# Loading two weight matrices from GpSimd's DMA queue with the fp16 conversion in the transfer

## The chip, the cores and the metric

One core of one Trainium2 chip runs the whole program. The metric is device time in microseconds, the median of the runs. Inputs and output are fp32 in DRAM; the matmuls work on bf16 and fp16 tiles on the chip.

## The reference, cut to what matters

Attention with a decay per position feeds a gated convolutional feed-forward block. Eight batches, eight heads, 576 positions, head size 64, so d_model is 512 and d_ff is 1024.

```python
scores = scale * q @ k.T                          # per batch and head, 576 x 576
decay  = cumsum(log(clip(f)))[:, None] - cumsum(log(clip(f)))[None, :]
attn   = softmax(where(causal, -1e9, scores + decay))
x      = (attn @ v)                               # heads side by side: [8, 576, 512]
h      = maximum(x @ w_in, 0)                     # [8, 576, 1024]
conv   = sum(conv_w[k] * h shifted by k - 1, k = 0..2)
out    = (h * sigmoid(conv)) @ w_out              # [8, 576, 512]
```

`w_in` is 512 x 1024 and `w_out` 1024 x 512, each 2 MB in fp32. Both are read once and used for all eight batches.

## The kernel before, in words

Everything is done on the one core in one pass. The attention is worked in 16 half batches of four heads (hb 0 to 15), the feed-forward in 8 batches (b 0 to 7), each as soon as its two half batches are through. The order of all work is written out by hand: the string ORDER lists some thousand steps, and each engine and each DMA queue gets its instructions in the order in which the steps stand there. An instruction waits only for its own data, but what stands behind it on its engine waits with it.

The steps that matter here, by their names in ORDER:

- `q2.0`, `q3.1` and the like (L233) load q or k of one half batch by a transposing DMA on SP's queue into one of four `qk` tiles. `cl` (L239, VectorE) then repairs the rows that carry the decay, and `rw` (L255, L256, SP) writes the decay rows into the tile.
- `v1.0` to `v1.4` (L262, SP) load v of batch 1 in five pieces into one of two `vf` tiles. `va2.0` and `va2.1` (L270, L272) convert them to fp16 on whichever engine ORDER names: `@POOL`, `@DVE` or `@ACT`.
- `sd`, `st`, `so` are score matmuls (L362, masks by L370), `ed`, `et`, `eo` the exponentials on ScalarE (L403, L382, L420).
- `pv` (L444, L448) is attention times v, `n` (L456, L458, VectorE) divides by the sums, `t` (L465, L467) turns the result, `tx` (L475) copies it out of PSUM.
- `f` (L484) is the first feed-forward matmul, `r` (L496) the relu, `c` and `d` (L503, L505) the convolution, `a` (L508) the tanh, `g` (L512) the gate, `o` (L523) the second matmul, `e` (L529) its eviction to an `ob` tile and `s` (L557) the store.
- `ki` (L328) and `zc` (L332, L333) are small DMAs on GpSimd's queue that write the decay rows and constants to DRAM.

The weights come in eight pieces of 512 KB: `wi0` to `wi3` for w_in and `wo0` to `wo3` for w_out. Each piece is loaded in fp32 into one of the three `ob` tiles by a DMA on SP's queue (`stage`, L571), and then converted into its half of `w_in_f16` or `w_out_f16` by `stage_cast` (L579): six of the eight casts stand on GpSimd (`wic0`, `wic1`, `wic2`, `woc1`, `woc3`, `woc2`), one on VectorE (`wic3`) and one on ScalarE (`woc0`). A piece of w_in holds two of the four row blocks for half of the columns: `f0.0` to `f0.3` need `wi0` and `wi1`, `f0.4` to `f0.7` need `wi2` and `wi3`. A piece of w_out holds two of the eight row blocks: `o0.0` starts with the blocks of `wo0` and needs all four pieces.

Of the kernel before, what the change touches and what calls it, by code (L numbers as in the profile page):

```python
# [19 lines left out]
q2.1 cl1.0.1@DVE cw ed0 cl1.1.1@DVE so0.1 v0.2 rw1 so0.0 eo0.0 q2.0 sd1 eo0.1 so1.0 ed1 cl2.1 cwt v0.4 wi3@SP eo1.0  # L20
va1.0@DVE sd3 ed3 cl2.0 sd2 st0 ed2 so2.0 va0.0@POOL va0.1@POOL eo2.0 q3.0 so2.1 wi0@SP wic0@POOL so1.1 eo2.1 so3.0
cl3.0 wic3@DVE so3.1 et0 va1.1@DVE eo1.1 rw2 pv0.0 eo3.1 st1 pv0.1 et1 sd4 q3.1 n0.0 n0.1 t0 wi1@SP eo3.0 pv1.0 q5.0
tx0@ACT pv1.1 cl3.1 n1.0 sd5 ed4 so5.0 n1.1 t1 tx1@DVE wic1@POOL so5.1 so4.1 wi2@SP rw3 ed5 eo5.1 f0.0 so4.0 q5.1
eo5.0 r0.0@ACT f0.1 st2 v1.0 q4.0 cl5.0 eo4.1 c0.0 d0.0 v1.2 eo4.0 r0.1@ACT f0.2 c0.1 v1.1 et2 sd6 cl5.1 r0.2@ACT c0.2
ed6 d0.1 h0 wic2@POOL a0.0 f0.3 so6.1 rw5 d0.2 eo6.1 r0.3@ACT a0.1 g0.0 c0.3 a0.2 g0.2 f0.4 f0.5 f0.6 f0.7 r0.5@ACT
v1.3 va2.0@POOL q4.1 r0.4@ACT sd7 so7.1 c0.5 cl4.0 c0.4 d0.4 ed7 so7.0 g0.1 r0.6@ACT eo7.1 sd10 so6.0 v1.4 eo7.0
wo2@SP r0.7@DVE eo6.0 a0.4 sd11 d0.3 so10.1 ed11 va3.0@POOL pv3.0 cl4.1 ed10 eo10.1 st3 d0.5 c0.6 so11.0 et3 wo1@SP
n3.0 a0.5 rw4 so11.1 wo3@SP va3.1@ACT pv2.0 eo11.1 c0.7 va2.1@POOL eo11.0 q6.0 pv2.1 v2.0 q6.1 woc1@POOL n2.0 n2.1
d0.7 sd9 ed9 pv3.1 so10.0 n3.1 a0.3 t2 wo0@SP g0.3 sd8 eo10.0 ed8 a0.7 t3 so9.0 v2.3 tx2@DVE tx3@DVE st5 eo9.0 g0.4
st4 d0.6 g0.5 v2.2 f1.0 et4 et5 so8.0 g0.7 f1.1 cl6.0 v2.1 r1.0@ACT eo8.0 woc3@POOL so8.1 c1.0 woc2@POOL f1.2 a0.6  # L30
cl6.1 v2.4 r1.1@ACT eo8.1 f1.3 v3.0 d1.0 r1.2@ACT g0.6 h1 r1.3@DVE a1.0 k0@POOL f1.4 so9.1 f1.5 rw6 q7.0 woc0@ACT zc
# [79 lines left out]
def kernel(  # L111
# [11 lines left out]
    nc = tc.nc  # L123
# [75 lines left out]
    add = plan.add  # L199
# [564 lines left out]
```

## Time and profile before

| what | value |
|---|---|
| median of three runs | 250.42 us (249.34 to 254.94) |
| span of the profiled execution | 246.3 us |
| median less span | 4.1 us |
| TensorE busy, matmul | 227.3 us, 92% |
| VectorE busy | 218.8 us, 89% |
| ScalarE busy | 209.2 us, 85% |
| GpSimd busy | 66.7 us, 27% |
| granted TensorE clock | full, in all slices |
| weight DMAs on SP's queue | 8, of 512 KB each |
| packets on the software queue (GpSimd's) | 304, 0.73 MB |

The page gives the span of the profiled execution and no separate time for it; the three runs lie around a median 4.1 us above that span. The profile names a tile by the kernel's names, "SPq" and "POOLq" are the queues' sequencers, q1 is the hardware DMA queue that SP feeds and q0 the software queue that GpSimd feeds. The number in square brackets behind a row of a timeline is the time in which the engine sat idle before it, and what ended that.

### The profile page before, as it was taken

Reading aid. Unit: us, or ns where it says so; the run is one execution under the profiler, and the core shown is the slowest. Engines: PE = TensorE matmul, PEld = TensorE weight load, DVE = VectorE, ACT = ScalarE, POOL = GpSimd, SP = SyncE. Lnnn points to the kernel's source line nnn. Section 1 sums busy time; section 2 is a strip of 40 time slices with the busy share of each in tenths; the row PEclk is TensorE's granted clock in tenths of the full one; section 3 lists DMA queues with packets and bytes.
Section 4 is the critical chain, followed back from the end, with each engine's and each line's share of the span. In section 5 each row is a group of like instructions: output and inputs, shape, how many; then the busy total and the mean of one; then the engine's idle time right before and its main releaser. Section 6 shows DMA issues by size and latency. Waiting matters only on the chain.

```text
span 246.3 us, 6458 instructions
## 1 busy us (share of the span) xinstructions
PE 227.3 (92%) x2644; PEld 145.0 (59%) x2644; DVE 218.8 (89%) x334; ACT 209.2 (85%) x282; POOL 66.7 (27%) x94
## 2 busy tenths in 40 slices
PE   0889979978999999989999999999999999999993
PEld 0777765557656755666557666665566566544441
DVE  6846285999998999999999999999999999999972
ACT  3558849999998999999999999989998999869641
POOL 8302022033423310550625244045234022001110
PEclk9999999999999999999999999999999999999999
DMA  6998999999999979899999999999999506334336
GB/s 163 335 238 195 225 204 212 225 179 287 210 238 226 231 169 213 165 230 225 237 230 225 243 235 205 185 245 192 280 208 198 159 1 92 104 118 170 101 124 202
DMA packets 116421, 48.80 MB, mean 198 GB/s; under 512 B 106290, under 2 KB 106546, under 8 KB 116392
## 3 DMA queue, kind: packets, MB, share of 16 engines
q1 hardware_dynamic: 115778, 47.24, 89.1%
q0 software_dynamic: 304, 0.73, 1.0%
q10 hardware_dynamic: 310, 0.42, 0.6%
q8 instruction: 20, 0.33, 0.6%
q14 instruction: 9, 0.07, 0.1%
HBM read 21.11 MB, written 10.17 MB: 127 GB/s over the span
## 4 chain that ended last, share of the span: by engine, by line
PE 49%; DVE 17%; ACT 14%; DMA 8%; issue 5%; SPq 4%; POOL 1%; ACTq 0%; DVEq 0%
PE ps L523 16%; PE ps L484 16%; PE ps L362 9%; DVE hg L512 4%; PE ps L444 4%; ACT pp L420 4%; DMA qk<-in_q_dram 3%; DVE u L505 3%; DVE u L503 3%; DMA vf<-in_v_dram 3%; ACT ht L496 3%; SPq L233 2%; DVE qk L227 2%; DMA hg<-in_q_dram 2%; DVE xm L458 2%
## 5 line engine op out<-in xcount | busy, mean ns | idle before, releaser
L484 PE MATMUL ps<-xt,w_in_f 128*128 128x512 f16 (+1 forms) x512 | 69.3, 286 | 0.3 <-DVE xt L475 0.3
L420 ACT ACTIVATE pp<-ps 128x1024 f16<-128x1024 f32 x64 | 64.5, 1035 | 4.2 <-PE ps L367 2.8
L362 PE MATMUL ps<-qk 128*128 128x128 bf16 (+2 forms) x576 | 62.1, 240 | 2.9 <-DVE xm L458 1.4
L523 PE MATMUL ps<-w_out_f,hg 128*128 128x512 f16 x256 | 59.9, 379 | 0.4 <-ACT ht L496 0.2
L505 DVE SCALAR_TENSOR_TENSOR u<-ht,cwt,u 128x576 f32<-128x576 f16 x64 | 53.7, 850 | 0.5
L503 DVE SCALAR_TENSOR_TENSOR u<-ht,cwt 128x576 f32<-128x576 f16 x64 | 52.2, 831 | 2.0 <-ACT ht L496 1.8
L508 ACT ACTIVATE hg<-u,cw 128x576 f16<-128x576 f32 x64 | 49.5, 788 | 4.5 <-DVE u L505 4.5
L362 PEld LDWEIGHTS <-qk 128*128 128x128 bf16 x576 | 38.7, 98 | 20.7 <-issue 4.5
L512 DVE SCALAR_TENSOR_TENSOR hg<-hg,ht 128x576 f16<-128x576 f16 x64 | 50.6, 811 | 0.3 <-POOL pt L385 0.3
L484 PEld LDWEIGHTS <-w_in_f 128*128 128x128 f16 x512 | 34.0, 98 | 28.1 <-issue 0.4
L523 PEld LDWEIGHTS <-hg 128*128 128x128 f16 x256 | 23.9, 98 | 26.6 <-issue 0.6
L496 ACT ACTIVATE ht<-ps 128x576 f16<-128x576 f32 x55 | 35.8, 665 | 1.8 <-PE ps L484 1.1
L406 POOL TENSOR_SCALAR_AFFINE_SELECT pp<-pd 128x1024 f16<-128x1024 f32 x20 | 25.3, 1279 | 43.1 <-ACT pd L403 34.4
L444 PE MATMUL ps<-va,pp 128*128 128x65 f16 x640 | 24.6, 193 | 1.3 <-POOL va L270 0.9
L458 DVE TENSOR_TENSOR xm<-ps,rc 128x896 f16<-128x896 f32 (+1 forms) x32 | 24.3, 758 | 1.1
L444 PEld LDWEIGHTS <-pp 128*128 128x128 f16 x640 | 22.7, 97 | 3.6 <-issue 1.7
L403 ACT ACTIVATE pd<-ps 128x1024 f32<-128x1024 f32 x20 | 20.3, 1026 | 1.7 <-issue 1.1
L239 DVE TENSOR_SCALAR qk<-qk,lim 128x2304 uint16<-128x2304 uint16 x12 | 10.8, 906 | 10.0 <-DMA qk<-in_q_dram 7.6
L529 ACT COPY ob<-ps 128x1024 f32<-128x1024 f32 (+1 forms) x17 | 16.1, 947 | 1.6 <-PE ps L523 1.3
L385 POOL TENSOR_SCALAR_AFFINE_SELECT pt<-p 128x256 f16<-128x256 f32 x10 | 8.4, 854 | 26.8 <-ACT p L382 19.6
L517 POOL COPY tl<-hg 128x64 f16<-128x64 f16 (+1 forms) x6 | 4.2, 694 | 38.1 <-DVE hg L512 38.1
L403 ACT ACTIVATE pp<-ps 128x1024 f16<-128x1024 f32 x12 | 12.1, 1030 | 1.7 <-PE ps L362 1.7
(93 smaller groups left out, 212.3 us busy)
## 6 DMA issues: line engine op xcount, KB each, us to landing
vf<-in_v_dram SPq DMA_DIRECT2D x32, 256.0 KB
out_dram<-ob SPq DMA_DIRECT2D x14, 512.0 KB
qk<-blank SPq DMA_DIRECT2D x8, 540.0 KB
ob<-in_moe_w_in_dram SPq DMA_DIRECT2D x4, 512.0 KB
ob<-in_moe_w_out_dram SPq DMA_DIRECT2D x4, 512.0 KB
vf<-in_v_dram SPq DMA_DIRECT2D x8, 128.0 KB
out_dram<-ob SPq DMA_DIRECT2D x8, 128.0 KB
out_dram<-ob SPq DMA_DIRECT2D x3, 256.0 KB
```

The lines of the kernel that those rows point to most:

```text
L362: nc.tensor.matmul(o, tk[:, h * S + k0:h * S + k0 + 128], tq[:, h * S + q0:h * S + q0 + n], start=first, stop=last and not by_matmul(hb, h))
L403: nc.scalar.activation(o, ps_of(f"sd{i}").rearrange("p (s c) -> p s c", s=2), AF.Exp, scale=SCALE)
L420: nc.scalar.activation(pair(i)[:, s, 512:1536], ps_of(f"so{i}.{s}"), AF.Exp, scale=SCALE)
L444: nc.tensor.matmul(ps[:, c:c + D + 1], block(hb, h, m, n), va[:, h, m, 0:D + 1], start=(m == 0), stop=(m == n))
L458: nc.vector.tensor_tensor(x.rearrange("p (j h d) -> p j h d", j=a, d=D), got[:, :, :, 0:D], r.unsqueeze(3).broadcast_to((128, a, g, D)), o ...
L484: nc.tensor.matmul(ps[:, c:c + n], w_in_f16[:, cc, 128 * ff:128 * (ff + 1)], xt[:, cc // 2, x:x + n], start=(cc == 0), stop=(cc == NCC - 1))
L496: nc.scalar.activation(o, i, AF.Relu, scale=0.5)
L503: nc.vector.scalar_tensor_tensor(u, ht[:, 0:S], cwt[:, ff, 0:1], ht[:, 1:1 + S], op0=ALU.mult, op1=ALU.add)
L505: nc.vector.scalar_tensor_tensor(u, ht[:, 2:2 + S], cwt[:, ff, 1:2], u, op0=ALU.mult, op1=ALU.add)
L508: nc.scalar.activation(hg_of(b, ff), u_t[slot[f"c{b}.{ff}", "u"]], AF.Tanh, scale=cw[:, ff, 1:2])
L512: nc.vector.scalar_tensor_tensor(hv, hv, 1.0, ht_of(b, ff)[:, 1:1 + S], op0=ALU.add, op1=ALU.mult)
L523: nc.tensor.matmul(ps[:, 512 * (c % 2):512 * (c % 2 + 1)], w, w_out_f16[:, ff, :], start=(ff == 0), stop=(ff == NFF - 1))
```

## The change

The eight steps `wi0` to `wi3` and `wo0` to `wo3` become DMAs on GpSimd's queue that read fp32 from DRAM and write fp16 straight into the weight tiles. The eight casts and their use of the `ob` tiles are gone. The matmuls wait for the DMAs themselves instead of the casts. V is loaded and converted as it was. In ORDER the steps keep their places; `wic` and `woc` are struck out.

```diff
-    def stage(w, j, e):
-        ob = ob_t[slot[f"{w}{j}", "ob"]].rearrange("p j c -> p (j c)").rearrange("p (x c) -> p x c", x=2)
+    def load_w(w, j):
         if w == "wi":
-            src = moe_w_in.rearrange("(cc p) ff -> p cc ff", p=128)[:, 2 * (j % 2):2 * (j % 2) + 2,
-                                                                    512 * (j // 2):512 * (j // 2) + 512]
+            x, y = 2 * (j % 2), 512 * (j // 2)
+            nc.gpsimd.dma_start(w_in_f16[:, x:x + 2, y:y + 512],
+                                moe_w_in.rearrange("(cc p) ff -> p cc ff", p=128)[:, x:x + 2, y:y + 512])
         else:
-            src = moe_w_out.rearrange("(ffc p) dm -> p ffc dm", p=128)[:, 2 * j:2 * j + 2, :]
-        queue(e).dma_start(ob, src)
-
-    def stage_cast(w, j, e):
...
-        {"ACT": nc.scalar.copy, "POOL": nc.gpsimd.tensor_copy, "DVE": nc.vector.tensor_copy}[e](dst, ob)
+            nc.gpsimd.dma_start(w_out_f16[:, 2 * j:2 * j + 2, :],
+                                moe_w_out.rearrange("(ffc p) dm -> p ffc dm", p=128)[:, 2 * j:2 * j + 2, :])
...
-            add(f"{w}{j}", "SP/POOL/ACT", [], lambda e, w=w, j=j: stage(w, j, e), take=["ob"])
-            add(f"{w}c{j}", "POOL/ACT/DVE", [f"{w}{j}"], lambda e, w=w, j=j: stage_cast(w, j, e), give=[("ob", f"{w}{j}")])
+            add(f"{w}{j}", "POOL", [], lambda w=w, j=j: load_w(w, j))
...
-            add(f"f{b}.{ff}", "PE", [f"tx{2 * b}", f"tx{2 * b + 1}"] + [f"wic{2 * (ff // 4) + j}" for j in range(2)],
+            add(f"f{b}.{ff}", "PE", [f"tx{2 * b}", f"tx{2 * b + 1}"] + [f"wi{2 * (ff // 4) + j}" for j in range(2)],
...
-        wo = [f"woc{j}" for j in range(4)]
+        wo = [f"wo{j}" for j in range(4)]
```

Three places show how the instructions move; line numbers are those of each kernel, the new one being two lines shorter up to the weight functions and eleven behind them. The first is SP's queue from the load of q for half batch 3 (`q3.0`, into qk_88) to the first loads of v for batch 1 (vf_90); ob_130 to ob_132 are the three fp32 tiles. Before:

```order
L571 DMA ob_130<-in_moe_w_in_dram 128x2x512
L233 DMA_TRANSPOSE qk_88<-in_q_dram 128x2304
L571 DMA ob_131<-in_moe_w_in_dram 128x2x512
L255 DMA qk_87<-image 1x2304
L256 DMA qk_87<-image 2x2304
L233 DMA_TRANSPOSE qk_88<-in_k_dram 128x2304
L571 DMA ob_132<-in_moe_w_in_dram 128x2x512
L233 DMA_TRANSPOSE qk_86<-in_q_dram 128x2304
L571 DMA ob_131<-in_moe_w_in_dram 128x2x512
```

And now:

```order
L231 DMA_TRANSPOSE qk_88<-in_q_dram 128x2304
L253 DMA qk_87<-image 1x2304
L254 DMA qk_87<-image 2x2304
L231 DMA_TRANSPOSE qk_88<-in_k_dram 128x2304
L231 DMA_TRANSPOSE qk_86<-in_q_dram 128x2304
```

Four weight loads are gone from between the loads of q and k. The four of w_out are gone in the same way further down that queue.

The second place is GpSimd's own order, from `ki` through the conversions of v for batch 0 (into va_92) and batch 1 (into va_93 and va_94) to the last of the weight steps. Before:

```order
L328 DMA image<-kc 64x576 x3
L270 CAST va_92<-vf_89 128x4x4x64
L272 CAST va_92<-vf_89 64x4x64
L579 CAST w_in_f_69<-ob_131 128x2x512
L579 CAST w_in_f_69<-ob_132 128x2x512
L579 CAST w_in_f_69<-ob_131 128x2x512
L270 CAST va_93<-vf_90 128x4x4x64
L270 CAST va_94<-vf_90 128x4x4x64
L272 CAST va_93<-vf_90 64x4x64
L579 CAST w_out_f_70<-ob_132 128x1024
L579 CAST w_out_f_70<-ob_131 128x1024
L579 CAST w_out_f_70<-ob_130 128x1024
```

And now:

```order
L326 DMA image<-kc 64x576 x3
L565 DMA w_in_f_69<-in_moe_w_in_dram 128x2x512
L268 CAST va_92<-vf_89 128x4x4x64
L270 CAST va_92<-vf_89 64x4x64
L565 DMA w_in_f_69<-in_moe_w_in_dram 128x2x512 x3
L268 CAST va_93<-vf_90 128x4x4x64
L568 DMA w_out_f_70<-in_moe_w_out_dram 128x2x512
L268 CAST va_94<-vf_90 128x4x4x64
L568 DMA w_out_f_70<-in_moe_w_out_dram 128x2x512 x2
L270 CAST va_93<-vf_90 64x4x64
L568 DMA w_out_f_70<-in_moe_w_out_dram 128x2x512
```

`wi3` now goes out right behind `ki`; `wi0`, `wi1`, `wi2` stand behind the two conversions of v for batch 0; `wo2` stands between `va2.0` (va_93) and `va3.0` (va_94), `wo1` and `wo3` ahead of `va2.1`, and `wo0` behind it.

The third place is VectorE from `cl3.0` (into qk_88) over `va1.1` (into va_91) to the first `n` step (`n0.0`, into xm_109). Before:

```order
L239 TENSOR_SCALAR qk_88<-qk_88,lim 128x2304
L579 CAST w_in_f_69<-ob_130 128x2x512
L272 CAST va_91<-vf_89 64x4x64
L456 RECIPROCAL rc_111<-ps_136 128x14
L458 TENSOR_TENSOR xm_109<-ps_136,rc_111 128x896
```

And now:

```order
L237 TENSOR_SCALAR qk_88<-qk_88,lim 128x2304
L270 CAST va_91<-vf_89 64x4x64
L454 RECIPROCAL rc_111<-ps_136 128x14
L456 TENSOR_TENSOR xm_109<-ps_136,rc_111 128x896
```

The cast of the weights between `cl3.0` and `va1.1` is gone; the rest keeps its order.

109 lines of the change are left out of this document (51 added, 58 removed).

## The prediction

> **What bounds the kernel now.** I read the busy time of each engine in stretches first, to see where an engine still idles.
>
> ```profile
> span 246.3 us, 6458 instructions
> 20.00:30.00 10.00, 9.86 (x128) 7.43 (x126) 3.84 (x10) 9.08 (x12) 1.43 (x2) 1.00 1.02 226
> 30.00:40.00 10.00, 8.10 (x145) 6.09 (x145) 7.08 (x13) 6.17 (x8) 2.12 (x2) 1.00 1.05 214
> 40.00:50.00 10.00, 9.99 (x93) 5.84 (x92) 9.04 (x12) 9.40 (x15) 1.50 (x1) 1.00 1.02 204
> 50.00:60.00 10.00, 7.98 (x135) 5.88 (x134) 9.56 (x13) 9.88 (x14) 3.47 (x4) 1.00 0.99 240
> 60.00:70.00 10.00, 9.55 (x138) 6.61 (x131) 9.90 (x17) 9.40 (x14) 3.58 (x3) 1.00 1.16 223
> 70.00:80.00 10.00, 9.45 (x107) 5.66 (x106) 8.99 (x14) 8.94 (x12) 3.68 (x7) 1.00 1.16 223
> 110.00:130.00 20.00, 20.00 (x207) 12.07 (x205) 19.55 (x28) 19.36 (x27) 5.54 (x5) 1.00 1.17 233
> ```
>
> The columns behind the length are the busy times of TensorE (PE), its weight loads, VectorE (DVE), ScalarE (ACT) and GpSimd (POOL), then granted clock, DMA share and GB/s. From 110 us on TensorE has no gap, and VectorE and ScalarE hardly any: nothing that this change touches works there, and a lead or a delay from before is carried to the end. All that can be won lies in the gaps from 20 to 80 us, where TensorE is idle for 60 less 54.9, or 5.1 us. DMA is busy throughout, and GpSimd is idle over 60% of each stretch, so its six casts cost nothing by their own length.
>
> Next I looked at who ends the gaps. The largest single one is at 32 us, and VectorE makes it:
>
> ```profile
> 33.26 0.78 PE L465 MATMUL ps<-ident,xm 128*128 128x128 f16 x8 [1.30 <-DVE xm L458]
> 29.40 0.88 DVE L239 TENSOR_SCALAR qk<-qk,lim 128x2304 uint16<-128x2304 uint16 x1 [5.99 <-DMA qk<-in_q_dram]
> 30.20 0.69 DVE L579 CAST w_in_f<-ob 128x1024 f16<-128x1024 f32 x1
> 30.80 1.13 DVE L272 CAST va<-vf 64x256 f16<-64x256 f32 x1
> 31.85 0.23 DVE L456 RECIPROCAL rc<-ps 128x14 f32<-128x14 f32 x1
> ```
>
> TensorE waits 1.30 us for `n0.0`. VectorE had been held 5.99 us by the load `q3.0`, then did the weight cast `wic3`, then `va1.1`, and only then `n0.0`.
>
> **The change part by part.** *VectorE at 30 us.* `wic3` goes: 0.69 us. `va1.1` also shortens, for it took four times its usual length while GpSimd cast `wic0` beside it:
>
> ```profile
> L272 DVE CAST va<-vf x3: 281/281/1127, 30.8 to 157.7; 64x256 f16<-64x256 f32 x3
> 30.70 1.09 POOL L579 CAST w_in_f<-ob 128x1024 f16<-128x1024 f32 x1 [6.86 <-DMA ob<-in_moe_w_in_dram]
> ```
>
> 1.13 less 0.28 is 0.85 us. Together `n0.0` comes 1.54 us earlier if `q3.0` lands when it did, and TensorE gains its whole idle 1.30 us.
>
> *SP's queue.* Eight issues leave it:
>
> ```profile
> L571 SPq DMA_DIRECT2D ob<-in_moe_w_in_dram x4: 524/586/620, 20.8 to 36.7; - x4
> L571 SPq DMA_DIRECT2D ob<-in_moe_w_out_dram x4: 399/567/683, 54.0 to 66.5; - x4
> 20.84 0.62 SPq L571 DMA_DIRECT2D ob<-in_moe_w_in_dram x1
> 21.51 4.26 SPq L233 DMA_TRANSPOSE qk<-in_q_dram  x1
> ```
>
> At the medians that is 4 x 0.586 + 4 x 0.567 = 4.6 us, 2.3 of it ahead of v for batch 1. `q3.0` goes out 0.67 us earlier and no longer behind 512 KB of `wi3`; but `wi3` now shares the DMA engines with the first loads of v, and `wi0` to `wi2` with `q3.0` and `q3.1`. I take these as even and leave `q3.0` where it was.
>
> *GpSimd's queue.* The nearest rows for an issue there are of 64 pieces of 1152 bytes each; the weights have 256 pieces of 2 KB.
>
> ```profile
> L328 POOL DMA_DIRECT2D image<-kc x3: 523/528/717, 7.9 to 9.1; - x3
> 53.36 2.55 POOL L270 CAST va<-vf 128x1024 f16<-128x1024 f32 x2 [9.73 <-DMA vf<-in_v_dram]
> 55.97 1.15 PE L444 MATMUL ps<-va,pp 128*128 128x65 f16 x32 [0.93 <-POOL va L270]
> ```
>
> An issue lies between 0.52 us (the row) and 2.1 us (four times it, by pieces). I take 1.0, an estimate nearer to the row, since one instruction's fixed part isn't paid per piece. This is no idle engine's own affair at one place: `wo2` now stands between `va2.0` and `va3.0`, and `pv3.0` already waited 0.93 us for `va3.0`. So `pv3.0` starts at 55.97 - d + i, where d is how much earlier v of batch 1 lands (0 if the DMA engines are the limit, 2.3 if SP's issues are; I take 2.0, because SP goes from one issue straight to the next, as from 20.84 over 21.46 to 21.51 above) and i the issue. That is 54.97, a lead of **1.0 us** of the 1.3; with the ends it runs from 1.8 us lead to 2.1 us loss.
>
> *ScalarE at 72 us.* `woc0` goes, 1.03 us, but ScalarE waited shortly after it:
>
> ```profile
> 72.39 1.03 ACT L579 CAST w_out_f<-ob 128x1024 f16<-128x1024 f32 x1
> 75.10 1.05 ACT L270 CAST va<-vf 128x1024 f16<-128x1024 f32 x1 [0.77 <-DMA vf<-in_v_dram]
> 78.52 0.82 DVE L503 SCALAR_TENSOR_TENSOR u<-ht,cwt 128x576 f32<-128x576 f16 x1 [0.94 <-ACT ht L496]
> ```
>
> If v for batch 2 doesn't land earlier, the cast becomes a longer wait and the gain is 0; if it does, 1.03 + 0.77 = 1.8 us. `wo1`, `wo3` and `wo0` leave SP ahead of it (about 1.7 us of issues). I take **0.5**, since VectorE has only its own 0.94 us of idle time to follow with.
>
> *When the weights land.* They must be there at these places:
>
> ```profile
> 39.05 1.14 PE L484 MATMUL ps<-xt,w_in_f 128*128 128x512 f16 x8
> 45.12 4.08 PE L484 MATMUL ps<-xt,w_in_f 128*128 128x512 f16 x32
> 73.47 3.61 PE L523 MATMUL ps<-w_out_f,hg 128*128 128x512 f16 x16 [0.16 <-ACT w_out_f L579]
> 23.44 0.40 POOL L272 CAST va<-vf 64x256 f16<-64x256 f32 x1 [2.40 <-DMA vf<-in_v_dram]
> 7.89 1.75 POOL L328 DMA_DIRECT2D image<-kc  x3 [0.99 <-DVE kc L322]
> ```
>
> `wi0` goes out at 23.8. The software queue is slow to start: of `ki`, issued from 7.89, the first packets ran in the 12th microsecond. I allow 2.5 us. `f0.0` needs 1.05 MB in 39.05 - 26.3 = 12.8 us, `f0.4` 1.57 MB in 18.8 us: 82 and 84 GB/s. `wo2` goes out behind `va2.0` at about 54.6, data from 57.1; `o0.0` needs 2.10 MB in 16.4 us: **128 GB/s**. What the queue moves beside transposes:
>
> ```profile
> q0 software_dynamic: 18, 0.05, 17.9%
> q0 software_dynamic: 37, 0.10, 30.8%
> q0 software_dynamic: 177, 0.43, 30.0%
> q0 software_dynamic: 74, 0.21, 70.3%
> ```
>
> These are packets, MB and share of the DMA engines in the windows 11 to 12, 12 to 13, 75 to 80 and 79 to 80 us: 100, 86 and at best 210 GB/s once running. I take 130, between 86 and 210, because 512 KB transfers keep the queue filled where 72 KB ones have pauses. Then `wo0` lands just as `o0.0` wants it, and costs 0; at 86 GB/s it takes 24.4 us and lands 8.0 us too late. What the conversion itself costs in the engines no row shows; the pace bounds it.
>
> The Trainium skill would decide this otherwise: "DMA: Bandwidth & Descriptors", section "Anatomy of one DMA — SWDGE (gpsimd) path", fits 2.0 us plus bytes over 436 GB/s, so by estimate 3.2 us for a piece and 6.8 us for four in a row. By that `o0.0` never waits and the sum stays; by the 86 GB/s row it is 255 to 256 us. The fit is for an otherwise idle set of engines, so I keep the rows.
>
> The sum: 246.3 - 1.0 - 0.5 = 244.8 us of span, and with the 4.1 us that the median lies above the span, **248.9 us**, against 250.42 before. Its own range is 246.8 to 250.4: both leads at their upper ends (1.8 + 1.8), or none.
>
> **The rivals.** *The software queue is too slow (slower than before).* One place, `o0.0`, decides, below 128 GB/s. For it speak the 86 GB/s of 75 to 80 us, against it the 210 of the last of these. At 105 GB/s `wo0` lands 3.6 us late, at 86 8.0; 1.0 of it is covered by the earlier start, and 1.7 (0.77 + 0.94) by ScalarE's and VectorE's idle time, so 251.3 to 255.7 us. Chance 0.24, of which 0.10 beyond 255.4.
>
> *Descriptors wait for VectorE.* GpSimd and VectorE got into each other's way above (1.13 against 0.28 us). If each of the four `wo` issues waits for one VectorE instruction like the 0.88 us `cl`, `wo0` is 4 x 0.88 = 3.5 us late; less the 2.7 us of cover named above that is 0.8, and with up to 0.9 at `pv3.0` 251.2 to 252.1 us. Against it: the small issues all took 0.52 to 0.72 us. Chance 0.12. The Trainium skill, "SBUF — State Buffer", section "Who interferes with whom", states this lock of a shared port; the stretched `va1.1` agrees with it, but no run here shows the writing of descriptors held up.
>
> *Issues cost 2.1 us on GpSimd.* Then `va2.1`, behind three of them, is the next to watch:
>
> ```profile
> 56.31 0.47 POOL L272 CAST va<-vf 64x256 f16<-64x256 f32 x1 [0.40 <-DMA vf<-in_v_dram]
> 61.46 0.32 PE L448 MATMUL ps<-va,pp 128*64 128x65 f16 x8
> ```
>
> The lead at `pv3.0` is gone (55.97 - 2.0 + 2.1), and `va2.1` moves to 56.3 - 2.0 + 6.3 = 60.6 and ends at 61.1, just before `pv2.1` reads it at 61.46; only ScalarE's 0.5 stays: 249.9 us. Chance 0.10.
>
> *SP's relief frees everything.* All 5.1 us of TensorE's gaps close: 245.3 us. Against it: several gaps are ended by ScalarE, not by a load. Chance 0.12, half of it below 245.4.
>
> **How the numbers follow.** Forecast 0.42, the rivals 0.24, 0.12, 0.10 and 0.12. Two per cent of 250.42 is 5.0 us, about what a measurement of this kernel can tell from no change: below 245.4 lies half of the last rival, 0.06; above 255.4 lie 0.10 of the first and 0.03 for a conversion slower than any row, 0.13; within, 0.81. The range 245.8 to 255.2 leaves out these two ends and little more.
>
> **What would show it.** In the profile after, TensorE's wait of 1.30 us at 33 us should be gone and `va1.1` take 0.28 us. `pv3.0` should start near 55.0. The software queue should show about 4.2 MB more read, and a weight issue near 1 us on GpSimd. If the first matmul on w_out starts later than 73.5 us and a DMA is what it waited for, the first rival is right; if a weight DMA's issue on GpSimd is stretched beside a VectorE instruction, the second; if `f0.0` waits for w_in, the pace is below 82 GB/s and the prediction is wrong at both places.

## The result, and the profile after

The changed kernel takes **259.7 us** (median of 4 runs, 256.29 to 260.13), the kernel before 249.88 us on the same chip (4 runs, 247.94 to 254.94): a ratio of 1.0396, interval 1.0305 to 1.0487. It is slower by about 10 us. Some executions of one and the same kernel run longer at a lower granted clock than its others; here and below medians are over all executions, ratios and their 95% intervals over the others alone. Forecast were 248.9 us and a range of 245.8 to 255.2.

The span of the profiled execution grew from 246.3 to 258.1 us. The stretches of the changed kernel, with the columns as in the prediction (TensorE, its weight loads, VectorE, ScalarE, GpSimd, granted clock, DMA share, GB/s):

```profile
20.00:30.00 10.00, 9.73 (x128) 7.27 (x126) 4.52 (x11) 9.08 (x13) 3.55 (x5) 1.00 1.05 172
30.00:40.00 10.00, 5.24 (x117) 4.13 (x117) 3.00 (x7) 4.11 (x5) 0.00 (x0) 0.99 1.51 156
40.00:50.00 10.00, 8.15 (x55) 4.77 (x55) 5.38 (x9) 4.71 (x6) 0.00 (x0) 0.67 0.90 172
50.00:60.00 10.00, 9.32 (x86) 5.55 (x84) 9.64 (x11) 9.39 (x15) 3.75 (x4) 1.00 0.77 158
60.00:70.00 10.00, 7.75 (x162) 6.12 (x160) 9.76 (x16) 8.82 (x12) 2.07 (x4) 1.00 1.06 163
110.00:130.00 20.00, 19.32 (x229) 12.44 (x222) 19.61 (x31) 18.98 (x26) 7.86 (x6) 1.00 1.07 213
130.00:150.00 20.00, 17.92 (x239) 12.00 (x237) 18.39 (x25) 16.29 (x23) 6.31 (x6) 0.91 1.15 212
```

From 30 to 40 us TensorE now idles for half of the time, and from 40 to 50 its clock is 0.67 where it was 1.00. From 30 to 40 us the busy share of the DMA engines rose from 1.05 to 1.51, while the GB/s fell from 214 to 156. That fall is one of counting: the page counts a converting DMA by the bytes it writes, and GpSimd's queue wrote 0.59 MB in that stretch, so read 1.18. With these the engines moved 2.15 MB, against 2.14 before. What changed is the order: from 28 to 30 us GpSimd's queue moved 189 packets and SP's queue 3. VectorE's timeline shows whom the other engines wait for:

```profile
29.73 0.88 DVE L237 TENSOR_SCALAR qk<-qk,lim 128x2304 uint16<-128x2304 uint16 x1 [4.47 <-DMA qk<-in_q_dram]
30.53 0.28 DVE L270 CAST va<-vf 64x256 f16<-64x256 f32 x1
30.73 0.23 DVE L454 RECIPROCAL rc<-ps 128x14 f32<-128x14 f32 x1
...
39.56 0.88 DVE L237 TENSOR_SCALAR qk<-qk,lim 128x2304 uint16<-128x2304 uint16 x1 [6.93 <-DMA qk<-in_k_dram]
```

And before, the last of these steps:

```profile
33.67 0.87 DVE L239 TENSOR_SCALAR qk<-qk,lim 128x2304 uint16<-128x2304 uint16 x1
```

`cl3.1`, the clamp of the transposed k of half batch 3, starts at 39.56 us instead of 33.67, 6.93 us of that spent waiting for the load `q3.1`. Behind it on VectorE stand `n1.0`, `n1.1` and the copy `tx1`, and so the first feed-forward matmuls of batch 0. TensorE's timeline:

```profile
32.14 0.78 PE L463 MATMUL ps<-ident,xm 128*128 128x128 f16 x8 [0.40 <-DVE xm L456]
...
41.77 1.01 PE L360 MATMUL ps<-qk 128*128 128x64 bf16 x4 [6.13 <-DVE xm L456]
...
45.47 1.72 PE L482 MATMUL ps<-xt,w_in_f 128*128 128x512 f16 x8
...
80.73 1.46 PE L521 MATMUL ps<-w_out_f,hg 128*128 128x512 f16 x6
```

The 1.30 us of idle time at 33.26 us became 0.40 at 32.14; predicted was that it goes whole. Then TensorE idles 6.13 us for VectorE, `f0.0` starts at 45.47 (39.05 before) and its eight matmuls take 1.72 us (1.14 before), and `o0.0` starts at 80.73 (73.47 before). Neither had a weight to wait for.

On SP's queue the load in question was issued when it always was, but the issue itself takes longer, and so does the next one:

```profile
27.34 5.27 SPq L231 DMA_TRANSPOSE qk<-in_k_dram  x1
32.72 6.65 SPq L231 DMA_TRANSPOSE qk<-in_q_dram  x1
```

Before, these two took 3.25 and 5.11 us, and `wi1` and `wi2` stood behind `q3.1` on the same queue:

```profile
27.47 3.25 SPq L233 DMA_TRANSPOSE qk<-in_k_dram  x1
30.76 0.59 SPq L571 DMA_DIRECT2D ob<-in_moe_w_in_dram  x1
31.46 5.11 SPq L233 DMA_TRANSPOSE qk<-in_q_dram  x1
36.69 0.52 SPq L571 DMA_DIRECT2D ob<-in_moe_w_in_dram  x1
```

In the new kernel `wi0`, `wi1` and `wi2` went out on GpSimd's queue one after the other, at 26.44, 27.2 and 27.9 us, so two of them ahead of the issue of `q3.1` at 27.34 and the third in its midst, for GpSimd has nothing else to do.

### The profile page after: what moved, and what is told of

It reads as the page before. It is cut to its first block, busy times and chain, and to the rows that moved or that the text cites. A ratio compares the mean times of both kernels' runs of the same rounds, so it can differ in the third digit from the quotient of the medians.

```text
span 258.1 us, 6451 instructions
## 1 busy us (share of the span) xinstructions
PE 231.0 (89%) x2644; PEld 147.1 (57%) x2644; DVE 221.6 (86%) x333; ACT 209.4 (81%) x281; POOL 63.8 (25%) x96
## 3 DMA queue, kind: packets, MB, share of 16 engines
q0 software_dynamic: 2480, 2.83, 6.6%
HBM read 21.11 MB, written 10.17 MB: 121 GB/s over the span
## 4 chain that ended last, share of the span: by engine, by line
PE 47%; DVE 22%; SPq 9%; DMA 9%; issue 6%; ACT 5%; ACTq 0%; DVEq 0%
PE ps L482 16%; PE ps L521 16%; PE ps L360 9%; DVE hg L510 5%; DVE u L503 5%; SPq L231 5%; DMA qk<-in_k_dram 5%; DVE u L501 4%; DVE xm L456 3%; PE ps L442 3%; SPq L260 3%; ACT pp L418 3%; DMA vf<-in_v_dram 2%; DMA hg<-in_q_dram 2%; PE ps L463 2%
## 5 line engine op out<-in xcount | busy, mean ns | idle before, releaser
L360 PE MATMUL ps<-qk 128*128 128x128 bf16 (+2 forms) x576 | 64.3, 245 | 11.6 <-DVE xm L456 9.5
L418 ACT ACTIVATE pp<-ps 128x1024 f16<-128x1024 f32 x64 | 64.7, 1037 | 12.3 <-DVE xt L473 7.9
L482 PE MATMUL ps<-xt,w_in_f 128*128 128x512 f16 (+1 forms) x512 | 71.0, 290 | 1.5 <-DVE ht L496 1.3
L503 DVE SCALAR_TENSOR_TENSOR u<-ht,cwt,u 128x576 f32<-128x576 f16 x64 | 56.6, 896 | 0.5
L360 PEld LDWEIGHTS <-qk 128*128 128x128 bf16 x576 | 39.8, 99 | 30.1 <-issue 14.6
L482 PEld LDWEIGHTS <-w_in_f 128*128 128x128 f16 x512 | 34.7, 99 | 30.4 <-issue 3.2
L510 DVE SCALAR_TENSOR_TENSOR hg<-hg,ht 128x576 f16<-128x576 f16 x64 | 51.5, 825 | 0.5 <-ACT hg L506 0.5
L521 PEld LDWEIGHTS <-hg 128*128 128x128 f16 x256 | 23.8, 98 | 26.0 <-DVE hg L510 0.3
L404 POOL TENSOR_SCALAR_AFFINE_SELECT pp<-pd 128x1024 f16<-128x1024 f32 x20 | 24.0, 1214 | 46.8 <-ACT pd L401 37.1
L237 DVE TENSOR_SCALAR qk<-qk,lim 128x2304 uint16<-128x2304 uint16 x12 | 11.1, 935 | 15.4 <-DMA qk<-in_k_dram 10.7
L268 POOL CAST va<-vf 128x1024 f16<-128x1024 f32 x5 | 6.6, 1329 | 45.6 <-DMA vf<-in_v_dram 43.4
```

The costliest lines, as they stand in the source:

```text
L360: nc.tensor.matmul(o, tk[:, h * S + k0:h * S + k0 + 128], tq[:, h * S + q0:h * S + q0 + n], start=first, stop=last and not by_matmul(hb, h))
L404: nc.gpsimd.affine_select(pair(i)[:, :, 0:512].rearrange("p s (m j) -> p s m j", j=128), pd_t[slot[f"ed{i}", "pd"]].rearrange("p s (m j) - ...
L418: nc.scalar.activation(pair(i)[:, s, 512:1536], ps_of(f"so{i}.{s}"), AF.Exp, scale=SCALE)
L482: nc.tensor.matmul(ps[:, c:c + n], w_in_f16[:, cc, 128 * ff:128 * (ff + 1)], xt[:, cc // 2, x:x + n], start=(cc == 0), stop=(cc == NCC - 1))
L503: nc.vector.scalar_tensor_tensor(u, ht[:, 2:2 + S], cwt[:, ff, 1:2], u, op0=ALU.mult, op1=ALU.add)
L510: nc.vector.scalar_tensor_tensor(hv, hv, 1.0, ht_of(b, ff)[:, 1:1 + S], op0=ALU.add, op1=ALU.mult)
```

## The experiments

Two theories at first. A: the burst of three pieces on a second queue holds SP's transposing loads up; then it makes the loss with w_in alone, also without conversion. B: the conversion in the transfer takes the engines' time. Later A was divided: is it GpSimd's queue, any second queue, or the moment? Edits are shown as changes of ORDER; only the steps concerned are named, and steps between them are left out, also where no dots stand. In the rows shown, kernels derived from the kernel before have its line numbers.

### One matrix at a time

Only w_out over GpSimd's queue (w_in as before), and only w_in (w_out as before):

```diff
-wo2@SP  wo1@SP  wo3@SP  wo0@SP   woc1@POOL woc3@POOL woc2@POOL woc0@ACT
+wo2     wo1     wo3     wo0
```

> Only the four pieces of w_out go over GpSimd's queue with conversion; w_in is loaded on SP's queue and cast as before. Theory A (the software queue's burst of wi0 to wi2 starves the transposing load q3.1, and that alone makes the loss): VectorE waits for q3.1 no longer than before (under 1 us), o0.0 starts at 72 to 74 us, the whole takes 246 to 250 us, ratio 0.985 to 1.00. Theory C (a good part of the loss is made behind 80 us by w_out or by GpSimd and VectorE in each other's way): 252 us or more.

Measured: 254.99 us (249.82 to 256.35, 4 runs) against 252.5 (247.53 to 254.75) before in that comparison; no interval could be given, so the time doesn't show whether w_out's pieces alone cost anything. The profile is that of the execution of 249.82 us. In it `cl3.1` is back at 33.68 us and `f0.0` at 38.35, but `o0.0` starts at 75.61, not at the expected 72 to 74. The burst of w_out has a victim of its own, the decay rows that `rw` loads on SP's queue for half batch 4; from 56 to 61 us SP's queue moved 6 packets and GpSimd's 748. TensorE's timeline:

```profile
61.87 0.61 PE L362 MATMUL ps<-qk 128*128 128x128 bf16 x4 [1.66 <-DMA qk<-image]
```

And the stretch from 60 to 65 us:

```profile
60.00:65.00 5.00, 3.34 (x41) 2.42 (x41) 2.63 (x6) 1.76 (x3) 0.00 (x0) 0.67 1.32 164
```

TensorE has 3.34 us of work at a clock of 0.67, where the kernel before has 4.84 at 1.00.

```diff
-wi3@SP  wi0@SP  wi1@SP  wi2@SP   wic0@POOL wic3@DVE wic1@POOL wic2@POOL
+wi3     wi0     wi1     wi2
```

> Only the four pieces of w_in go over GpSimd's queue with conversion; w_out as before. Theory A: VectorE waits 5 to 8 us for q3.1, TensorE idles about 6 us from 35 us on with a lower granted clock behind it, and the whole takes 256 to 260 us, ratio 1.03 to 1.05. Theory C: 252 us or less, since half of the loss belongs to w_out.

Measured: 256.9 us (254.4 to 258.31), ratio 1.0233 (0.9932 to 1.0534). The interval holds 1, so by the time alone the loss is not shown here. The wait is there with w_in alone, and longer, in VectorE's timeline of an execution of 258.31 us:

```profile
40.93 0.88 DVE L239 TENSOR_SCALAR qk<-qk,lim 128x2304 uint16<-128x2304 uint16 x1 [9.29 <-DMA qk<-in_k_dram]
```

### The same queue without conversion

w_in goes over GpSimd's queue in fp32 into `ob` tiles (four instead of three), and all casts stay; `wi1` and `wi2` stand beside `wi0`:

```diff
-wi3@SP   wi0@SP   wi1@SP   wi2@SP
+wi3@POOL wi0@POOL wi1@POOL wi2@POOL
```

> The four pieces of w_in go over GpSimd's queue at the same places as in e2, but in fp32 into the ob tiles (one tile more), without conversion; the casts on GpSimd and VectorE and all of w_out as before. Theory A (the queue and the moment make the loss): q3.1 takes 10 us or more to land again and the whole takes 255 to 260 us. Theory B (the conversion in the transfer makes its packets slow and blocks the transposes): q3.1 lands within 7 us of its issue and the whole takes 248 to 252 us.

Measured: 261.44 us (260.98 to 263.77), ratio 1.0512 (1.0355 to 1.0669). `cl3.1` in VectorE's timeline:

```profile
44.63 1.47 DVE L239 TENSOR_SCALAR qk<-qk,lim 128x2304 uint16<-128x2304 uint16 x1 [13.12 <-DMA qk<-in_k_dram]
```

Without the conversion the loss is there all the same, so theory B falls as its cause. That it is larger than with the conversion isn't shown, since the two intervals overlap.

### The same pieces earlier

```diff
-ki@POOL ... wi3 ... wi0 ... wi1 ... wi2
+ki@POOL wi3 wi0 wi1 wi2
```

> As the changed kernel, but wi0, wi1 and wi2 go out right behind wi3 at about 10 us, ahead of the first conversions of v. Theory A: they share the engines with the first loads of v and of half batch 2 instead of q3.1; VectorE has 6 us to spare there, so the wait for q3.1 goes and the whole takes 246 to 252 us. If any burst of 1.5 MB costs the same wherever it falls, some load of q, k or v lands 5 us late between 12 and 25 us and the whole takes 254 us or more. Theory B says the latter as well.

Measured: 255.66 us (254.75 to 257.75), ratio 1.0283 (1.007 to 1.0496). The wait moved to the transposing load that was under way then, `q2.1`, as VectorE's timeline shows:

```profile
23.40 0.88 DVE L237 TENSOR_SCALAR qk<-qk,lim 128x2304 uint16<-128x2304 uint16 x1 [6.61 <-DMA qk<-in_k_dram]
```

Before, `cl2.1` started at 19.11 us after a wait of 2.06. `cl3.1` now starts at 35.79 without a wait, and `f0.0` at 41.56, 2.5 us late instead of 6.4. The time is not the 246 to 252 us that theory A expected: three pieces in a row cost something at this place too, and more was lost from 130 to 150 us, at a stretched step of VectorE that is told below with the second profile of the changed kernel.

### Pieces held back

A copy of one column on GpSimd reads what a clamp has written; the weight loads behind it on GpSimd's queue can't start earlier:

```diff
+    def hold(x, hb, side):
+        nc.gpsimd.tensor_copy(scr[:, x:x + 1], (stq_t, stk_t)[side][hb % RING][:, 0:1])
...
-q3.0 so2.1 wi0 ... t0 wi1 ... so4.1 wi2 ...           wo2 ... wo1 ... wo3 ... wo0
+q3.0 so2.1 wi0 ... cl3.1 hx0 wi1 wi2 ... cl5.0 hx1 wo2 cl5.1 hx2 wo1 cl4.0 hx3 wo3 cl4.1 hx4 wo0
```

> The changed kernel with its pieces held back: a copy of one column on GpSimd, which reads what cl3.1 has written, stands ahead of wi1 and wi2, and one such copy each behind cl5.0, cl5.1, cl4.0 and cl4.1 stands ahead of wo2, wo1, wo3 and wo0. Nothing else differs. Theory of order (the loads share engines that are full; what cost time is only that three pieces overtook q3.1 and four overtook the rows of rw4 and q6): cl3.1's wait of 6.93 us falls under 1 us, TensorE's clock is 1.00 from 40 to 50 us, f0.0 starts between 39 and 41 us (wi1 issued near 34.5, landing 5.9 us later), and the time is 248 to 251 us. Theory of the software queue (its packets hold the others up wherever they stand): cl3.1's wait goes too, but cl5.0, cl5.1 or cl4.0 wait 2 us or more in its place, and the time is 253 to 257 us.

Measured: 256.56 us, ratio 1.0197 (1.0094 to 1.03). Its profile spans 391.8 us at a clock of 0.57, so the stages are read from a second profile of this kernel, further down. The second kernel differs only in which piece goes at which place, the first near 10 us, the next near 26:

```diff
-wi3 ... q3.0 so2.1 wi0 ... cl3.1 hx0 wi1 wi2
+wi0 ... q3.0 so2.1 wi1 ... cl3.1 hx0 wi2 wi3
```

> As the kernel with all pieces held, but with the pieces of w_in renamed: wi0 goes first (near 10 us), wi1 next (near 26 us), and wi2 and wi3, which f0.4 is the first to need, are held behind cl3.1. Theory of order: no wait over 1 us at cl3.1 or f0.0, f0.0 at 38 to 39.5 us, f0.4 not waiting for a weight, and 247 to 250 us, at or under the kernel before. Theory of the software queue: a wait of 2 us or more at cl3.1, cl5.0 or cl5.1, and 252 to 256 us.

Measured: 251.08 us (10 runs) against 251.99 (25 runs), ratio 0.9996 (0.9946 to 1.0046). With one piece ahead of `q3.1` instead of three, `f0.0` starts at 38.60 us and `cl3.1` here:

```profile
33.94 0.88 DVE L237 TENSOR_SCALAR qk<-qk,lim 128x2304 uint16<-128x2304 uint16 x1 [2.13 <-DMA qk<-in_k_dram]
```

So with conversion and queue as in the change, the order and the moment of the pieces bring the time back to that of the kernel before. It takes the right order, though: the first kernel has one piece ahead of `q3.1` as well and lost 2% all the same.

### Another queue, before and behind the load

Is it GpSimd's queue? ScalarE has a hardware queue of its own (q10). First the three pieces in fp32 on that queue, behind `eo2.0`:

```diff
-eo2.0 ... wi0@POOL ... wi1@POOL wi2@POOL
+eo2.0 wi0@ACT wi1@ACT wi2@ACT
```

> The kernel that loaded w_in in fp32 over GpSimd's queue and kept the casts, with one difference: wi0, wi1 and wi2 are issued by ScalarE (behind eo2.0, near 24 us) on its hardware queue. Theory of order (any queue that overtakes costs the same): cl3.1 waits 9 to 14 us as there, and the time is 258 to 264 us. Theory of the software queue (GpSimd's queue alone is served ahead of SP's): the two hardware queues share, cl3.1 waits under 4 us, and the time is 250 to 255 us.

Measured: 251.03 us (11 runs), ratio 0.9975 (0.993 to 1.0021). No loss: `f0.0` starts at 38.67. VectorE's clamp `cl3.1`, and ScalarE's issue of the three pieces:

```profile
33.03 1.60 DVE L239 TENSOR_SCALAR qk<-qk,lim 128x2304 uint16<-128x2304 uint16 x1
```

```profile
26.70 1.45 ACTq L571 DMA_DIRECT2D ob<-in_moe_w_in_dram  x3
```

Taken alone this speaks for GpSimd's queue as the culprit. But ScalarE issued the pieces from 26.70 us, 1.5 us behind `q3.1` (25.23), where GpSimd had been 0.9 ahead of it. So the moment was moved with the queue, and the next kernel moved it back:

```diff
-eo1.0 ... eo2.0 wi0@ACT wi1@ACT wi2@ACT
+eo1.0 wi0@ACT wi1@ACT wi2@ACT ... eo2.0
```

> The kernel with wi0, wi1 and wi2 in fp32 on ScalarE's hardware queue, with one difference: the three are issued behind eo1.0, near 24 to 25.5 us, so ahead of q3.1's issue (25.23 there; the pieces followed it at 26.70). Theory of the software queue (only GpSimd's queue holds the transposing loads up): cl3.1 waits under 3 us, the clock stays at 1.00 from 35 to 50 us, 249 to 254 us. Theory of the moment (on any second queue, pieces ahead of q3.1 hold it up, pieces behind it don't): cl3.1 waits 5 us or more, the clock falls under 0.9 in that stretch, 256 to 262 us.

Measured: **259.4 us** (259.13 to 262.58), ratio 1.0426 (1.032 to 1.0532), the loss of the change without its queue and without its conversion. ScalarE's timeline has the issues of the three pieces, SP's the issue of `q3.1`, VectorE's the clamp `cl3.0`:

```profile
22.23 1.54 ACTq L571 DMA_DIRECT2D ob<-in_moe_w_in_dram  x3
```

```profile
26.60 13.35 SPq L233 DMA_TRANSPOSE qk<-in_k_dram  x1
```

```profile
40.08 0.88 DVE L239 TENSOR_SCALAR qk<-qk,lim 128x2304 uint16<-128x2304 uint16 x1 [15.58 <-DMA qk<-in_q_dram]
```

The pieces stand ahead of the end of `q3.0`, whose clamp comes 10.7 us late, and `q3.1` needs 13.35 us only to be issued. What the queues moved from 25 to 35 us (packets, MB, share of the engines), first with the pieces ahead of the loads, then with them behind:

```profile
DMA packets 2153, 1.51 MB, mean 151 GB/s; under 512 B 1624, under 2 KB 1624, under 8 KB 2152
q10 hardware_dynamic: 558, 1.08, 63.4%
q1 hardware_dynamic: 1594, 0.41, 46.7%
```

```profile
DMA packets 3739, 2.33 MB, mean 233 GB/s; under 512 B 2967, under 2 KB 2967, under 8 KB 3738
q1 hardware_dynamic: 2923, 0.74, 58.9%
q10 hardware_dynamic: 815, 1.57, 43.3%
```

In the second kernel the two queues ran one after the other: in the microsecond from 33 to 34 the weights had the engines alone, and moved 0.40 MB; the transposing loads alone, in the kernel before from 26 to 27 us, moved 1134 packets. The two rows, from the queues' view of each kernel:

```profile
q10 hardware_dynamic: 209, 0.40, 106.7%
```

```profile
q1 hardware_dynamic: 1134, 0.29, 127.6%
```

At these rates the traffic of the first kernel would take 1594 / 1134 + 1.08 / 0.40 = 4.1 us; it took the 10, of which one (32 to 33 us) was nearly idle. By the same estimate the second kernel's traffic needs 2923 / 1134 + 1.57 / 0.40 = 6.5 us of its 10. So the interleaved streams got 41% of the rate that they have alone, the others 65%. The loss needs neither GpSimd's software queue nor the conversion.

The mirror of that pair is GpSimd's queue behind the load, in fp32, held until `cl3.0`:

```diff
-so2.1 wi0@POOL wi1@POOL wi2@POOL wic0@POOL ... cl3.0
+so2.1 ... cl3.0 hx0 wi0@POOL wi1@POOL wi2@POOL wic0@POOL
```

> The kernel with w_in in fp32 over GpSimd's queue and the casts kept, with one difference: a copy of one column on GpSimd that reads what cl3.0 has written holds wi0, wi1 and wi2 until about 27 us, 1 us behind q3.1's issue, as they stood on ScalarE's queue. Theory of the software queue: cl3.1 or cl5.0 still waits 4 us or more for its load, 255 to 262 us. Theory of the moment: q3.1 comes through first, cl3.1 and cl5.0 wait under 2 us, 249 to 253 us.

Measured: 255.96 us, ratio 1.0232 (1.0122 to 1.0343). `cl3.1` starts at 31.99, earlier than in any other kernel, and `f0.0` at 37.77; the wait went to the next transposing loads, `q5.0` and `q5.1`, as VectorE's timeline shows:

```profile
46.05 0.88 DVE L239 TENSOR_SCALAR qk<-qk,lim 128x2304 uint16<-128x2304 uint16 x1 [8.77 <-DMA qk<-in_q_dram]
```

By the letter this is what the theory of the software queue expected. It doesn't decide between the queues, though: the held pieces went out from 29.32 us, 2.6 us later than on ScalarE's queue, and `q5.0` was issued at 30.24, in their midst. It does show that another transposing load can be the victim. Meeting one isn't enough, however: on ScalarE's queue behind the load, the pieces moved from 31 to 35 us with 49 packets of SP's queue beside them, just as `q5.0` was being issued (from 31.14), and `cl5.0` started at 39.09, ahead of the 40.19 of the kernel before.

### The pieces early on SP's own queue

```diff
-q3.0 so2.1 wi0@SP ... q3.1 ... wi1@SP ... wi2@SP
+q3.0 so2.1 wi0@SP wi1@SP wi2@SP ... q3.1
```

> The kernel before, with wi1 and wi2 issued by SP right behind wi0, so ahead of q3.1 on the same queue, and a fourth staging buffer; casts as before. Theory of order: q3.1 is issued behind two more pieces of 512 KB, which at the 211 GB/s of the stretch from 30 to 35 us take 2.5 us each, so cl3.1 waits 4 to 6 us, TensorE's clock falls under 0.9 somewhere from 35 to 50 us, and the time is 254 to 259 us. Theory of the software queue: on one hardware queue the pieces only take their own time, part of it in the slack of q3.1; cl3.1 waits under 3 us, the clock stays at 1.00, and the time is 249 to 253 us.

Measured: 253.16 us (10 runs), ratio 1.009 (1.0037 to 1.0142). `cl3.1` waits 2.41 us but starts at 38.96, as `cl3.0` before it had waited 7.70; `f0.0` at 43.67. On one queue no piece can overtake a load that stands ahead of it, and the two pieces put ahead of `q3.1` cost 5.3 us at `cl3.1` and 0.9% of the whole. My test by the wait at `cl3.1` was badly chosen, since a clamp that starts late hides its own wait; the starting times below are the better measure.

### The changed kernel once more, and w_in held alone

> The changed kernel itself, without an edit, to see whether the stretch from 110 to 150 us, where its profile lost some 4 us more, belongs to it. If that loss follows from the change (a lasting shift of GpSimd's masks against VectorE's steps): TensorE's clock is under 0.95 again in a stretch of 5 us between 110 and 150 us, the slowest L503 is over 2.5 us, and o0.0 to the end takes 4 us longer than before, as in the first profile. If it was that execution's alone: no such stretch, and the profiled span is 252 to 255 us. The wait at cl3.1 is expected at 5 to 9 us by both.

Measured: 257.0 us (254.31 to 257.99), ratio 1.0268 (1.0144 to 1.0391), span 255.9.

VectorE's timeline and the stretch from 40 to 45 us:

```profile
41.74 0.88 DVE L237 TENSOR_SCALAR qk<-qk,lim 128x2304 uint16<-128x2304 uint16 x1 [10.16 <-DMA qk<-in_k_dram]
```

```profile
40.00:45.00 5.00, 1.05 (x7) 0.69 (x7) 2.64 (x5) 0.00 (x0) 0.00 (x0) 0.50 0.77 119
```

The wait at `cl3.1` is there again, 10.16 us long and so longer than the 5 to 9 expected, and TensorE's clock is 0.50 behind it. From 30 to 40 us the engines moved less this time, 1.58 MB with the weights counted as read. From 110 to 150 us TensorE's clock is 1.00 in every 5 us, and a step of VectorE that was stretched in the first profile isn't. By source line, first profile and second:

```profile
L503 DVE SCALAR_TENSOR_TENSOR u<-ht,cwt,u x11: 805/812/3043, 113.1 to 147.9; 128x576 f32<-128x576 f16 x11
L503 DVE SCALAR_TENSOR_TENSOR u<-ht,cwt,u x13: 804/819/960, 109.1 to 149.4; 128x576 f32<-128x576 f16 x13
```

So the loss there doesn't follow from the change as such. Nor does it belong to that one execution: a step of 3.05 us, beside the same run of casts and masks on GpSimd, stands in three other profiles too (w_in early, all pieces held, two pieces on ScalarE's queue), with 1.6 to 2.0 us less work of TensorE from 130 to 150 us. The last of them has no converting load, so this loss depends on how the steps of the two engines come to lie.

Then only w_in in the held order, w_out on SP's queue with its casts:

```diff
-wi3@SP ... wi0@SP ... wi1@SP ... wi2@SP   wic0@POOL wic3@DVE wic1@POOL wic2@POOL
+wi0 ... q3.0 so2.1 wi1 ... cl3.1 hx0 wi2 wi3
```

> Only w_in goes over GpSimd's queue with conversion, in the held order (wi0 near 10 us, wi1 near 25 us, wi2 and wi3 behind cl3.1); w_out is loaded in fp32 by SP and cast as before. With all eight pieces held, the stretch from 50 to 60 us had 6.82 us of TensorE at a clock of 0.83 against 7.97 us at 1.00 before. If w_out's pieces made that loss (between q4.0 and va2.0): TensorE is back at 7.9 us or more with a clock of 1.00 there, and the time is 248 to 250 us, 1 to 2 us under the kernel before. If w_in's held pieces made it: the loss stays, and the time is 250.5 to 252.5 us.

Measured: 248.96 us (10 runs, 247.8 to 251.37) against 250.97 (13 runs), ratio 0.9976 (0.993 to 1.0021). From 50 to 60 us TensorE has 7.95 us at a clock of 1.00, against 6.82 at 0.83 with all eight pieces held, so w_out's pieces made that loss. That it beats the kernel before isn't shown, since the interval holds 1.

### How the cost grows with the pieces

> The kernel with all pieces held (wi3 first, wi0 at its place, wi1 and wi2 behind cl3.1), for a profile by stage. If wi1 comes late for f0.0: cl3.1 waits under 3 us, f0.0 starts 2 us or more behind its twin's 38.60 us and waits for a load or stands behind it, and the span is 250 to 254 us. If the held pieces of w_out hold up q4 and q5: f0.0 is within 1 us of the twin's and VectorE waits 2 us or more at cl5 or cl4.

Measured: one execution, 252.14 us beside 251.14 for the kernel before. Neither branch holds: `f0.0` starts at 37.69, ahead of its twin, with a wait of 0.74 us for `wi1` in its midst, and the longest wait at `cl5` or `cl4` is 1.33. TensorE loses 1.6 us from 130 to 150 us, where the stretched step stands. Why this kernel's median was 5 us above its twin's is not settled.

Next, one or two of the three pieces on ScalarE's queue behind `eo1.0`, the others on SP's at their old places:

```diff
-eo1.0 wi0@ACT wi1@ACT wi2@ACT
+eo1.0 wi0@ACT           ... t0 wi1@SP ... so4.1 wi2@SP
```

> As the kernel with wi0, wi1 and wi2 on ScalarE's hardware queue behind eo1.0 (cl3.0 waited 15.58 us there), but with wi0 alone there; wi1 and wi2 are back on SP's queue at their places of the kernel before. In proportion: a third of it, so the waits at cl3.0 and cl3.1 are 4 to 6 us in all against 0.6 to 2 us where nothing overtakes, and the span is 249 to 252 us. A threshold: under 2.5 us in all, 246 to 249 us.

> The same with wi0 and wi1 on ScalarE's queue behind eo1.0 and wi2 on SP's. In proportion: waits of 8 to 11 us at cl3.0 and cl3.1, span 252 to 257 us. A threshold above two pieces: under 3 us, span 246 to 249 us.

Measured, one execution each: 250.84 and 255.51 us beside 251.14. The waits (6.05 and 5.23 us, both at `cl3.0`) don't tell the two theories apart, as the kernel before has 5.99 there too. The starts say more, each from one profiled execution:

| pieces ahead of `q3.1` on a second queue | `cl3.1` | `f0.0` |
|---|---|---|
| none (kernel before) | 33.67 | 39.05 |
| none, three behind it (ScalarE's queue) | 33.03 | 38.67 |
| none, three behind it (GpSimd's, fp32; these met `q5.0`) | 31.99 | 37.77 |
| one, ScalarE's queue | 34.09 | 40.89 |
| one, GpSimd's, converted (three kernels with held pieces) | 33.02 to 34.33 | 37.69 to 38.99 |
| two, ScalarE's | 34.94 | 40.32 |
| three, GpSimd's, converted (changed kernel, twice; w_in alone) | 39.56, 41.74, 40.93 | 45.47, 47.64, 46.84 |
| three, GpSimd's, fp32 | 44.63 | 50.75 |
| three, ScalarE's, fp32 | 44.34 | 50.99 |
| three, GpSimd's, converted, near 10 us (these met `q2.1`) | 35.79 | 41.56 |

One piece costs at most 0.7 us at `cl3.1`, two 1.3, three near the load 5.9 to 11.0: not in proportion. But number and moment weren't separated. The three pieces on ScalarE's queue were issued from 22.23 us, at the start of `q3.0`'s issue (21.79 to 25.41), the two from 24.06, near the end of it (24.74), and from 27 to 29 us they had the engines nearly alone, with 30 packets of SP's queue beside them. `f0.0` follows `cl3.1` by 4.7 to 6.8 us in every row, so `cl3.1` sets most of it. The kernel with two pieces lost its time later, at the stretched step: TensorE 18.03 us at a clock of 0.91 from 130 to 150 us.

## Why the prediction was wrong

*VectorE at 30 us: right but for 0.4 us.* `wic3` is gone, `va1.1` takes 0.28 us, `n0.0` starts at 30.73 instead of 31.85, and TensorE's idle time before `t0` fell from 1.30 to 0.40. `n0.0` came 1.12 us earlier instead of 1.54, as `cl3.0` before it came 0.33 later.

*SP's queue: the step that failed.* I wrote that `wi0` to `wi2` share the engines "with `q3.0` and `q3.1`. I take these as even and leave `q3.0` where it was." `q3.0` stayed where it was (`cl3.0` at 29.73 against 29.40). `q3.1` did not: its clamp came 5.89 us late, 8.07 in the second profile, and TensorE's work on `f0.0` 6.4 and 8.6 us. I had put this at nothing. I had counted which issues leave SP's queue, but not that the queue had been what kept `wi1` and `wi2` behind `q3.1`. On GpSimd, idle at that point, all three went out within 2.2 us, and their data went ahead of it. The pair on ScalarE's queue shows that this is enough: the same three pieces behind the load cost nothing (0.9975), ahead of it 4.3% (1.0426). "Even" can be wrong a second time: in the early one of that pair the interleaved streams got only 41% of their separate rates. The changed kernel didn't need that for its loss. By the same estimate, with 0.19 MB written per microsecond for GpSimd's queue alone (below), its traffic from 30 to 40 us needs 3708 / 1134 + 0.59 / 0.19 = 6.4 us of the 10 in the first profile, about the 6.5 of the pieces behind the load. In the second, with 2778 packets and 0.43 MB, it is 4.7, and `cl3.1` came later.

A smaller miss stands ahead of it: `wi0` went out at 26.44 us, not at 23.8, as the conversion of v that it stands behind came at 26.10 instead of 23.44. The `wi3` that I let share the engines "with the first loads of v" had moved from 20.84 us on SP's queue to 9.62. In the profiles with one piece at that early place `cl2.1` starts at 19.4 to 20.6 us, in the three without at 19.0 to 19.2.

The Trainium skill, "DMA: Bandwidth & Descriptors", section "Issuing engines are not separate DMA queues", says that DMAs of all issuing engines run on the same 16 DMA engines and interleave, so that a second issuer saves only the issue time. The traces agree that the engines are shared: the clamps move with either second queue. They add what the rule doesn't say, on the pair with ScalarE's queue: 151 GB/s interleaved against 233 in the same ten microseconds one after the other.

*The clock: missing.* I had no term for a stall that lasts. After 6.13 and 9.34 us without work TensorE's clock was 0.50 from 40 to 45 us in both profiles. In the first `f0.0` followed `cl3.1` by 5.91 us instead of 5.38 and took 1.72 instead of 1.14: about 1.1 us more. "TensorE: Matmul & The Clock Gate" of the Trainium skill, Part 1, halves the clock after an idle window of some 3.4 us; the 0.50 agrees.

*The account.* In the second profile `f0.0` is 8.6 us late, `o0.0` (82.17 against 73.47) 8.7, and the span 9.6: nearly the whole loss stands at `f0.0` and is carried to the end, as the prediction said of any delay. In the first `f0.0` is 6.4 us late, `o0.0` 7.3, and the span 11.8; most of the other 4.5 us fell in 110 to 150 us, at the stretched step. From `o0.0` to the end the second execution lost 0.9. I had written that nothing which the change touches works behind 110 us; how the steps of VectorE and GpSimd come to lie against each other there can change, and that I had left out.

*GpSimd's queue: right in kind.* An issue costs 0.72 to 0.74 us at the median, where I took 1.0. From the view by source line:

```profile
L565 POOL DMA_DIRECT2D w_in_f<-in_moe_w_in_dram x4: 721/738/768, 9.6 to 27.9; - x4
L568 POOL DMA_DIRECT2D w_out_f<-in_moe_w_out_dram x4: 713/716/821, 57.8 to 61.4; - x4
```

That excludes the rival of 2.1 us, and with 0.82 at most also descriptors held up by VectorE. The lead at `pv3.0` and the 0.5 us at ScalarE couldn't be seen: `pv3.0` came at 63.41 instead of 55.97.

*When the weights land: the wrong fear.* `f0.0`, `f0.4` and `o0.0` never waited for a weight in the changed kernel. The queue I thought slow (130 GB/s, an estimate from small transfers) can have the engines to itself. In the kernel with w_in early, from 14 to 15 us, the queues moved:

```profile
q0 software_dynamic: 190, 0.19, 116.4%
q1 hardware_dynamic: 10, 0.00, 1.0%
```

That is 0.19 MB written and so 0.38 read per microsecond, about the 0.40 of the fp32 pieces on ScalarE's queue. My first rival was slower for the opposite reason: it ended on the right side, at the wrong place. None of the four rivals had the loads that are left on SP's queue as the victim; I had looked only at when the weights arrive, not at what they pass.

*The offset.* I added 4.1 us for what lies around the span. The changed kernel's profiled execution took 259.98 us with its span of 258.1, so 1.9 us; the rest was spread between executions. It changes nothing in the difference.

*What a right order would give.* With w_in held, the predicted gain of 1.5 us would be 0.6%; measured was a ratio of 0.9976, with an interval from a gain of 0.7% to a loss of 0.2%.

What stays open: why the interleaved streams lose so much of their rate in some places, when from 13 to 19 us (the kernel with w_in early) the weights ran at nearly their full rate, 0.97 MB written, past a held-up `q2.1`; whether GpSimd's queue is worse than ScalarE's at the same moment; and whether two pieces pass where three don't, at the same moment. The profile doesn't show what a DMA engine waits for inside a packet.

## What to carry to other kernels

A load moved from a busy in-order queue to an idle engine's queue is not only issued cheaper: it loses everything that stood ahead of it. Write down what it overtakes, and when that is wanted, before counting the saved casts and issues. Where the DMA engines are full, give a moved load a data dependency that puts it back in its place, one or two pieces at a time; here that turned a loss of 3 to 4% into no loss in two kernels of three (0.9996 and 0.9976), while the third, with its pieces in another order, kept 2%. And change queue and moment separately, as the run that moved both pointed to the wrong culprit.

## What the runs showed of the hardware

- Transposing loads and large plain loads on two queues, interleaved, moved 151 GB/s together over 10 us, against 0.29 and 0.40 MB per microsecond alone, and 233 GB/s one after the other; three pieces of 512 KB beside it delayed the clamp behind a transposing load by 5.9 to 11.0 us, two, issued at another moment, by 1.3.
- The conversion fp32 to fp16 in the transfer cost hardly any rate where it ran nearly alone: 0.38 MB read per microsecond, against 0.40 for fp32 without conversion. An issue of 128x2x512 elements took 0.71 to 0.77 us of GpSimd, 0.82 in one case.
- The page counts a converting DMA's bytes as written: q0 grew by 2.10 MB (0.73 to 2.83) for 4.2 MB of weights, while HBM read stayed at 21.11 MB. The prediction expected 4.2 MB there.
- The issue of a transposing load on SP stretches with the traffic: 1.91 to 13.35 us for the same instruction, `q3.1`.
- A VectorE step that takes 0.81 us at the median took 3.05 beside a run of casts and masks on GpSimd, in four of the profiles, whether weights were converted in the transfer or not.
